# Pooled attention followed by a snake MoE block: transposed layout throughout, batches interleaved, pooling by adds, DMAs from another queue

## The chip, the cores and the metric

One core of one Trainium2 chip. The metric is the device time of one execution in microseconds (us): the median of several executions. The profile is one execution, followed instruction by instruction. Its span runs from the first to the last instruction and is some 2 us shorter than the device time of the same execution.

Engines: PE multiplies matrices, PEld is its weight load, DVE (VectorE), ACT (ScalarE) and POOL (GpSimd) do element work, SP (sync) issues DMAs. Everything is float32.

## The reference

```python
# q, k, v: (8 batches, 8 heads, 576 tokens, 64)
def attn(q, k, v):
    k_p = k.reshape(B, H, 72, 8, 64).mean(axis=3)      # keys and values pooled by 8
    v_p = v.reshape(B, H, 72, 8, 64).mean(axis=3)
    scores = q @ k_p.transpose(0, 1, 3, 2) / sqrt(64)
    scores = scores - scores.max(-1, keepdims=True)
    a = exp(scores)
    a = a / (a.sum(-1, keepdims=True) + 1e-9)
    return a @ v_p

x = attn(q, k, v).transpose(0, 2, 1, 3).reshape(4608, 512)
h = x @ w_in                                            # 512 x 2048
g = h + sin(alpha * h) ** 2 / (alpha + 1e-9)            # alpha: 2048 values, one per column of h
out = g @ w_out                                         # 2048 x 512
```

## The kernel before

Attention runs head by head and query tile by query tile. Each tile is transposed back and written to DRAM; the MoE block reads it again and transposes it on PE, computes h with tokens on the partitions, and transposes h as well, so that the second product can contract over the 2048 columns.

```python
    for b in range(B):
        for h in range(H):
            ...   # loads of k, v, q of 128 tokens, pooling by a matmul with pm, transposes
            for (ms, mlen) in m_tiles:                       # 5 query tiles
                nc.tensor.matmul(sc_ps[:mlen], qt[:, ms:ms + mlen], kp[:], start=True, stop=True)
                ...   # copy, max, exp, sum, reciprocal, multiply: [tokens, 72]
                nc.tensor.transpose(attnT_ps[:, :mlen], attn[:mlen], ident[:mlen, :mlen])
                nc.vector.tensor_copy(out=attnT[:, :mlen], in_=attnT_ps[:, :mlen])
                nc.tensor.matmul(o_ps[:, :mlen], vp[:], attnT[:, :mlen], start=True, stop=True)
                nc.vector.tensor_copy(out=o_sb[:, :mlen], in_=o_ps[:, :mlen])
                nc.tensor.transpose(oT_ps[:mlen, :], o_sb[:, :mlen], ident[:D, :D])
                nc.vector.tensor_copy(out=oT[:mlen], in_=oT_ps[:mlen])
                nc.gpsimd.dma_start(out=x_dram[b, ms:ms + mlen, h, :], in_=oT[:mlen])
    ...   # weights and alpha are loaded here
    for ti in range(NT):                                     # 36 tiles of 128 tokens
        nc.gpsimd.dma_start(out=xc[:], in_=xf[ti * P:(ti + 1) * P, :])
        ...   # four transposes of xc into xT
        for nf in range(n_ff_tiles):
            for kk in range(K1):
                nc.tensor.matmul(h_ps[:], xT[:, kk, :], w_in_t[...], start=(kk == 0), stop=(kk == K1 - 1))
            nc.vector.tensor_copy(out=h_sb[...], in_=h_ps[:])
        for kk in range(K2):                                 # 16
            nc.tensor.transpose(hT_ps[:], h_sb[:, kk * P:(kk + 1) * P], ident[:])
            nc.vector.tensor_copy(out=hT[:], in_=hT_ps[:])
            ...   # sine on ACT, square, times 1/alpha, plus h: three more DVE instructions
            nc.tensor.matmul(out_ps[:], hT[:], w_out_t[:, kk, :], start=(kk == 0), stop=(kk == K2 - 1))
```

Of the kernel before, what the change touches and what calls it, by code (L numbers as in the profile page):

```python
# [13 lines left out]
AF = mybir.ActivationFunctionType  # L15



@with_exitstack
def kernel(  # L20
    ctx: ExitStack,
    tc: tile.TileContext,
    q: bass.AP,
    k: bass.AP,
    v: bass.AP,
    moe_w_in: bass.AP,
    moe_w_out: bass.AP,
    moe_alpha: bass.AP,
    out: bass.AP,
):  # L30
    nc = tc.nc
    B, H, S, D = q.shape
    pool = 8
    Sp = S // pool
    scale = 1.0 / (D ** 0.5)
    d_model = H * D
    N_tok = B * S
    d_ff = moe_w_in.shape[1]
    assert moe_w_in.shape == (d_model, d_ff)
    assert moe_w_out.shape == (d_ff, d_model)  # L40

    x_dram = nc.dram_tensor("x_bridge", (B, S, H, D), F32, kind="Internal").ap()

    P = 128

    singles = ctx.enter_context(tc.tile_pool(name="singles", bufs=1))
    ident = singles.tile([P, P], F32)
    make_identity(nc, ident)
    pm = singles.tile([P, P // pool], F32)
    nc.vector.memset(pm[:], 1.0 / pool)  # L50
    nc.gpsimd.affine_select(out=pm[:], in_=pm[:], pattern=[[-pool, P // pool]],
                            compare_op=mybir.AluOpType.is_ge, fill=0.0,
                            base=0, channel_multiplier=1)
    nc.gpsimd.affine_select(out=pm[:], in_=pm[:], pattern=[[pool, P // pool]],
                            compare_op=mybir.AluOpType.is_ge, fill=0.0,
                            base=pool - 1, channel_multiplier=-1)

    actx = ctx.enter_context(ExitStack())
    apool = actx.enter_context(tc.tile_pool(name="attn_sbuf", bufs=3))
    apsum = actx.enter_context(tc.tile_pool(name="attn_psum", bufs=4, space=bass.MemoryType.PSUM))  # L60

    m_tiles = []
    s0 = 0
    while s0 < S:
        m = min(P, S - s0)
        m_tiles.append((s0, m))
        s0 += m

    n_sc = S // P
    assert S % pool == 0  # L70

    for b in range(B):
        for h in range(H):
            kp = apool.tile([D, Sp], F32)
            vp = apool.tile([Sp, D], F32)
            vp_d = apool.tile([D, Sp], F32)
            qt = apool.tile([D, S], F32)
            off = 0
            sp_off = 0
            while off < S:  # L80
                clen = min(P, S - off)
                clen = (clen // pool) * pool
                kc = apool.tile([P, D], F32)
                vc = apool.tile([P, D], F32)
                qc = apool.tile([P, D], F32)
                nc.gpsimd.dma_start(out=kc[:clen], in_=k[b, h, off:off+clen, :])  # L86
                nc.gpsimd.dma_start(out=vc[:clen], in_=v[b, h, off:off+clen, :])  # L87
                nc.gpsimd.dma_start(out=qc[:clen], in_=q[b, h, off:off+clen, :])  # L88
                qcT_ps = apsum.tile([D, P], F32, tag="ps")
                nc.tensor.transpose(qcT_ps[:, :clen], qc[:clen], ident[:clen, :clen])  # L90
                nc.vector.tensor_copy(out=qt[:, off:off+clen], in_=qcT_ps[:, :clen])
                spc = clen // pool
                kp_ps = apsum.tile([D, P // pool], F32, tag="ps")
                vp_ps = apsum.tile([D, P // pool], F32, tag="ps")
                nc.tensor.matmul(kp_ps[:, :spc], kc[:clen], pm[:clen, :spc], start=True, stop=True)
                nc.tensor.matmul(vp_ps[:, :spc], vc[:clen], pm[:clen, :spc], start=True, stop=True)
                nc.vector.tensor_copy(out=kp[:, sp_off:sp_off+spc], in_=kp_ps[:, :spc])
                nc.vector.tensor_copy(out=vp_d[:, sp_off:sp_off+spc], in_=vp_ps[:, :spc])
                off += clen
                sp_off += spc  # L100
            vpT_ps = apsum.tile([Sp, D], F32, tag="ps")
            nc.tensor.transpose(vpT_ps[:], vp_d[:], ident[:D, :D])
            nc.vector.tensor_copy(out=vp[:], in_=vpT_ps[:])

            for (ms, mlen) in m_tiles:
                sc_ps = apsum.tile([P, Sp], F32, tag="ps")
                nc.tensor.matmul(sc_ps[:mlen], qt[:, ms:ms + mlen], kp[:], start=True, stop=True)  # L107
                sc = apool.tile([P, Sp], F32)
                nc.vector.tensor_copy(out=sc[:mlen], in_=sc_ps[:mlen])
                mx = apool.tile([P, 1], F32)  # L110
# [21 lines left out]
                nc.gpsimd.dma_start(out=x_dram[b, ms:ms + mlen, h, :],  # L132
                                    in_=oT[:mlen])

    actx.close()

    xf = x_dram.rearrange("b s h d -> (b s) (h d)")

# [83 lines left out]
```

## Time and profile before

| | before |
|---|---|
| device time, median | 3109.25 us (3108.4 to 3111.08, 4 runs of the comparison) |
| span of the profile | 3105.1 us |
| busy PE, DVE, ACT, POOL | 66%, 49%, 13%, 23% of the span |
| first stage, attention | to about 1940 us |
| second stage, MoE | 1947 to 3096 us |

A kernel with no engine fully busy can be bound in two ways, and this one has both, one after the other. The average of 66% for PE hides it; the 40 slices of the span, shown in the prediction, do not.

### The profile page before, as it was taken

How to read it: one execution, taken by the hardware profiler on the slowest of the kernel's cores; microseconds unless marked ns; L12 is line 12 of the kernel's file. 1: busy time of each engine (PE TensorE's matmuls, PEld its weight loads, DVE VectorE, ACT ScalarE, POOL GpSimd, SP SyncE). 2: the span in 40 equal slices, each digit the busy share in tenths (PEclk: the TensorE clock that was granted, in tenths of full speed). 3: DMA queues.
4: the chain of work that ended last, by engine and by line, in shares of the span. 5: the costliest groups of instructions: out<-in, count | busy, mean ns of one | idle time of the engine just before them, and what ended most of it. 6: DMA issues, size and time to landing. Idle time of an engine off the chain costs nothing.

```text
span 3105.1 us, 24590 instructions
## 1 busy us (share of the span) xinstructions
PE 2038.2 (66%) x6608; PEld 1024.8 (33%) x6608; DVE 1518.1 (49%) x6214; ACT 408.1 (13%) x1218; POOL 725.8 (23%) x1363
## 2 busy tenths in 40 slices
PE   4444444444444444444444444999999999999998
PEld 2222222222222222222222222344444444444443
DVE  3444444444444444444444443566565656656565
ACT  0100101000000100001000010122121212112121
POOL 4343333333333333333333332000000000000000
PEclk9999999999999999999999999999999999999999
DMA  0000000000000000000000001200000000000000
GB/s 25 17 26 26 20 22 18 22 19 21 20 19 22 17 22 19 21 21 19 23 17 23 19 21 45 89 17 21 14 14 21 14 21 14 21 14 14 21 11 10
DMA packets 48472, 66.66 MB, mean 21 GB/s; under 512 B 21712, under 2 KB 25808, under 8 KB 47824
## 3 DMA queue, kind: packets, MB, share of 16 engines
q0 software_dynamic: 48336, 65.11, 6.5%
q8 instruction: 54, 0.88, 0.1%
q14 instruction: 82, 0.67, 0.1%
HBM read 46.15 MB, written 18.87 MB: 21 GB/s over the span
## 4 chain that ended last, share of the span: by engine, by line
issue 45%; PE 34%; POOL 16%; DVE 3%; DMA 2%; ACT 1%; POOLq 0%
PE out_ps L187 15%; PE h_ps L171 14%; POOL x_bridge L132 5%; POOL kc L86 4%; POOL qc L88 4%; POOL vc L87 3%; PE hT_ps L178 2%; DVE h_sb L173 1%; DMA qc<-in_q_dram 1%; DMA kc<-in_k_dram 1%; PE o_ps L125 0%; DMA w_in_t<-in_moe_w_in_dram 0%; PE sc_ps L107 0%; PE attnT_ps L121 0%; PE xT_ps L164 0%
## 5 line engine op out<-in xcount | busy, mean ns | idle before, releaser
L187 PE MATMUL out_ps<-w_out_t,hT 128*128 128x512 f32 x1152 | 593.8, 629 | 1.1 <-DVE hT L186 0.8
L121 PE MATMUL attnT_ps<-ident,attn 128*72 128x128 f32 (+1 forms) x320 | 130.1, 406 | 626.3 <-DVE attn L119 626.3
L171 PE MATMUL h_ps<-w_in_t,xT 128*128 128x512 f32 x1152 | 515.3, 594 | 12.3 <-DMA w_in_t<-in_moe_w_in_dram 12.3
L132 POOL DMA_DIRECT2D x_bridge<-oT x320 | 173.2, 541 | 989.5 <-DVE oT L131 976.1
L182 ACT ACTIVATE s_t<-hT,alpha_t 128x128 f32<-128x128 f32 x576 | 227.1, 401 | 901.7 <-DVE hT L180 901.7
L171 PEld LDWEIGHTS h_ps<-w_in_t,xT 128*128 128x128 f32 x1152 | 218.0, 192 | 267.5 <-issue 267.3
L112 ACT ACTIVATE mx<-mx 128x1 f32<-128x1 f32 (+1 forms) x320 | 64.9, 203 | 1735.2 <-DVE mx L111 1735.2
L125 PE MATMUL o_ps<-attnT,vp 72*64 72x128 f32 (+1 forms) x640 | 206.4, 426 | 117.3 <-DVE attnT L123 117.3
L121 PEld LDWEIGHTS attnT_ps<-ident,attn 128*72 128x72 f32 (+1 forms) x320 | 43.2, 135 | 691.2 <-DVE attn L119 691.2
L173 DVE COPY h_sb<-h_ps 128x512 f32<-128x512 f32 x144 | 99.5, 691 | 342.3 <-PE h_ps L171 342.2
L187 PEld LDWEIGHTS out_ps<-w_out_t,hT 128*128 128x128 f32 x1152 | 181.2, 188 | 238.2 <-DVE hT L186 201.9
L88 POOL DMA_DIRECT2D qc<-in_q_dram x320 | 171.0, 534 | 230.6 <-PE qcT_ps L90 226.0
L160 POOL DMA_DIRECT2D xc<-x_bridge x36 | 19.6, 543 | 823.7 <-PE xT_ps L164 818.3
L127 DVE COPY o_sb<-o_ps 64x128 f32<-64x128 f32 (+1 forms) x320 | 86.2, 269 | 236.0 <-PE o_ps L125 236.0
L107 PE MATMUL sc_ps<-kp,qt 64*128 64x72 f32 (+1 forms) x640 | 196.9, 410 | 0.0
L129 PE MATMUL oT_ps<-ident,o_sb 64*128 64x64 f32 (+1 forms) x320 | 113.8, 355 | 116.1 <-DVE o_sb L127 116.1
L90 PE MATMUL qcT_ps<-ident,qc 128*64 128x128 f32 (+1 forms) x320 | 124.2, 388 | 90.5 <-DMA qc<-in_q_dram 88.3
L86 POOL DMA_DIRECT2D kc<-in_k_dram x320 | 175.5, 549 | 12.5 <-issue 5.4
L184 DVE TENSOR_TENSOR s_t<-s_t 128x128 f32<-128x128 f32 x576 | 167.7, 291 | 16.6 <-ACT s_t L182 14.2
L117 DVE TENSOR_REDUCE sm<-attn 128x1 f32<-128x72 f32 (+1 forms) x320 | 72.4, 226 | 210.3 <-ACT attn L114 210.3
L186 DVE TENSOR_TENSOR hT<-hT,s_t 128x128 f32<-128x128 f32 x576 | 166.9, 290 | 15.8
L87 POOL DMA_DIRECT2D vc<-in_v_dram x320 | 171.1, 535 | 5.9 <-issue 2.9
(45 smaller groups left out, 2276.5 us busy)
## 6 DMA issues: line engine op xcount, KB each, us to landing
xc<-x_bridge POOLq DMA_DIRECT2D x36, 256.0 KB, 2.9
out_dram<-o_sb POOLq DMA_DIRECT2D x36, 256.0 KB, 2.3
kc<-in_k_dram POOLq DMA_DIRECT2D x256, 32.0 KB, 2.0
vc<-in_v_dram POOLq DMA_DIRECT2D x256, 32.0 KB, 1.9
qc<-in_q_dram POOLq DMA_DIRECT2D x256, 32.0 KB, 1.9
x_bridge<-oT POOLq DMA_DIRECT2D x256, 32.0 KB, 1.7
w_in_t<-in_moe_w_in_dram POOLq DMA_DIRECT2D x1, 4096.0 KB, 13.5
w_out_t<-in_moe_w_out_dram POOLq DMA_DIRECT2D x1, 4096.0 KB, 22.0
```

The lines of the kernel that those rows point to most:

```text
L86: nc.gpsimd.dma_start(out=kc[:clen], in_=k[b, h, off:off+clen, :])
L87: nc.gpsimd.dma_start(out=vc[:clen], in_=v[b, h, off:off+clen, :])
L88: nc.gpsimd.dma_start(out=qc[:clen], in_=q[b, h, off:off+clen, :])
L107: nc.tensor.matmul(sc_ps[:mlen], qt[:, ms:ms + mlen], kp[:], start=True, stop=True)
L121: nc.tensor.transpose(attnT_ps[:, :mlen], attn[:mlen], ident[:mlen, :mlen])
L125: nc.tensor.matmul(o_ps[:, :mlen], vp[:], attnT[:, :mlen], start=True, stop=True)
L132: nc.gpsimd.dma_start(out=x_dram[b, ms:ms + mlen, h, :], in_=oT[:mlen])
L171: nc.tensor.matmul(h_ps[:], xT[:, kk, :], w_in_t[:, kk, nf * N_FF_TILE:(nf + 1) * N_FF_TILE], start=(kk == 0), stop=(kk == K1 - 1))
L182: nc.scalar.activation(out=s_t[:], in_=hT[:], func=AF.Sin, bias=0.0, scale=alpha_t[:, kk:kk + 1])
L184: nc.vector.tensor_mul(out=s_t[:], in0=s_t[:], in1=s_t[:])
L186: nc.vector.tensor_add(out=hT[:], in0=hT[:], in1=s_t[:])
L187: nc.tensor.matmul(out_ps[:], hT[:], w_out_t[:, kk, :], start=(kk == 0), stop=(kk == K2 - 1))
```

## The change

Its intent: keep the features on the partitions from attention to the end of the MoE block, so that nothing has to be transposed back or sent through DRAM; do attention for a whole batch at once; and put the attention of batch b+1 between the MoE steps of batch b, so that its latency lies under PE's matmuls. Pooling becomes three adds of halves, on GpSimd (DVE for the first batch's keys). DMAs are issued from sync.

The diff rewrites the file; its core:

```diff
-    for b in range(B):
-        for h in range(H):
-            ...
-            for (ms, mlen) in m_tiles:
-                ...
-                nc.tensor.transpose(oT_ps[:mlen, :], o_sb[:, :mlen], ident[:D, :D])
-                nc.gpsimd.dma_start(out=x_dram[b, ms:ms + mlen, h, :], in_=oT[:mlen])
+        # pooling: 8 -> 4 -> 2 -> 1 by adds
+        for n, eng in (("k", nc.vector if b == 0 else nc.gpsimd), ("v", nc.gpsimd)):
+            for i, t in enumerate(st[n]):
+                for w in (4 * D, 2 * D, D):
+                    eng.tensor_tensor(out=o, in0=t[:, :, 0:w], in1=t[:, :, w:2 * w], op=OP.add)
+        yield
+        # two heads per score matmul, by block-diagonal keys kb
+        for i, (t0, n) in enumerate(tiles):
+            for g in range(2):
+                for hh in range(2):
+                    nc.tensor.matmul(..., qt[:, hp, t0:t0 + n], kb[:, hp, :], start=True, stop=True)
+                ...   # max and subtract on DVE
+                yield
+        nc.scalar.activation(out=ex[:, 0:4], in_=ex[:, 0:4], func=AF.Exp, scale=scale)
+        nc.scalar.activation(out=ex[:64, 4], in_=ex[:64, 4], func=AF.Exp, scale=scale)
+        ...   # sums and reciprocals on DVE, multiply on GpSimd, transposes, copies
+        # output of attention, transposed: features on the partitions
+            for hp in range(NP):
+                for e in range(2):
+                    h = 2 * hp + e
+                    nc.tensor.matmul(ps[64 * e:64 * e + 64, :n], vp[:, h, :], aT[:, h, t0:t0 + n], start=True, stop=True)
+                nc.vector.tensor_copy(out=self.xT[c][:, hp, o:o + n], in_=ps[:, :n])
+                yield
-    for ti in range(NT):
-        nc.gpsimd.dma_start(out=xc[:], in_=xf[ti * P:(ti + 1) * P, :])
-        ...
-        for kk in range(K2):
-            nc.tensor.transpose(hT_ps[:], h_sb[:, kk * P:(kk + 1) * P], ident[:])
-            ...
+    def moe(self, c):                                  # a chunk of 384 tokens
+        for f in range(K2 + 2):
+            if f < K2:
+                for kk in range(K1):
+                    nc.tensor.matmul(ps[:], self.w_in_t[:, kk, f * P:(f + 1) * P], xT[:, kk, :], ...)
+                nc.scalar.activation(out=s[:], in_=ps[:], func=AF.Sin, scale=self.al[:, f:f + 1])
+                nc.scalar.activation(out=s[:], in_=s[:], func=AF.Square)
+                nc.vector.scalar_tensor_tensor(out=g[:], in0=s[:], scalar=self.ral[:, f:f + 1], in1=ps[:], ...)
+            if f >= 2:
+                for t in range(NT):
+                    nc.tensor.matmul(acc[t][:], gs[f - 2][:, t * P:(t + 1) * P], self.w_out_t[:, f - 2, :], ...)
+            yield
+            for cc in chunks:
+                for _ in self.moe(cc):
+                    for _ in range(4 if len(chunks) == 1 else 2):
+                        next(nxt, None)                # a piece of the next batch's attention
```

Below, an "f step" is one turn of the loop over f: 8 records of h and 6 of the output. A record is one entry of PE in the trace; a float32 matmul leaves two, a transpose one.

## The prediction

> **What bounds the kernel now.** I read the slices of the span first (busy tenths of each engine in 40 slices), then the table of stretches, then one tile of each stage in the timeline.
>
> ```profile
> PE   4444444444444444444444444999999999999998
> DVE  3444444444444444444444443566565656656565
> POOL 4343333333333333333333332000000000000000
> ```
>
> There are two stages one after the other: attention up to about 1940 us, in which no engine is half busy, and the MoE block, in which the PE has no gap. The table of stretches gives the same in numbers (busy us of each engine in 400 us of each stage):
>
> ```profile
> 1200.00:1600.00 400.00, 189.63 (x754) 111.27 (x754) 168.49 (x753) 37.35 (x134) 142.05 (x267) 1.00 0.06 20
> 2000.00:2400.00 400.00, 393.82 (x1056) 171.67 (x1055) 251.04 (x925) 80.48 (x204) 13.54 (x25) 1.00 0.05 17
> ```
>
> Attention, one query tile of one head in the timeline (start, duration, engine, what, and the idle time before it):
>
> ```profile
> 1011.81 0.20 ACT L112 ACTIVATE mx<-mx 128x1 f32<-128x1 f32 x1 [4.06 <-DVE mx L111]
> ...
> 1013.21 0.43 PE L121 MATMUL attnT_ps<-ident,attn 128*72 128x128 f32 x1 [1.96 <-DVE attn L119]
> 1013.67 0.29 DVE L123 COPY attnT<-attnT_ps 72x128 f32<-72x128 f32 x1 [0.52 <-PE attnT_ps L121]
> 1014.02 0.69 PE L125 MATMUL o_ps<-attnT,vp 72*64 72x128 f32 x2 [0.38 <-DVE attnT L123]
> 1014.74 0.28 DVE L127 COPY o_sb<-o_ps 64x128 f32<-64x128 f32 x1 [0.78 <-PE o_ps L125]
> 1015.08 0.36 PE L129 MATMUL oT_ps<-ident,o_sb 64*128 64x64 f32 x1 [0.37 <-DVE o_sb L127]
> ...
> 1016.00 0.55 POOL L132 DMA_DIRECT2D x_bridge<-oT  x1 [4.09 <-DVE oT L131]
> ...
> 1016.46 0.20 ACT L112 ACTIVATE mx<-mx 128x1 f32<-128x1 f32 x1 [4.05 <-DVE mx L111]
> ```
>
> It is a relay: each instruction starts when the one before has ended on another engine. The same step recurs 4.65 us later (1011.81 to 1016.46). 320 tiles x 4.65 = 1488 us; the remaining 450 us are 64 head openings of 7 us (loads, pooling, q transposes). So attention is latency, not work.
>
> MoE, steady state:
>
> ```profile
> 2499.83 0.19 PEld L171 LDWEIGHTS h_ps<-w_in_t,xT 128*128 128x128 f32 x1 [0.24 <-issue]
> 2500.26 0.19 PEld L171 LDWEIGHTS h_ps<-w_in_t,xT 128*128 128x128 f32 x1 [0.24 <-issue]
> 2500.69 0.19 PEld L171 LDWEIGHTS h_ps<-w_in_t,xT 128*128 128x128 f32 x1 [0.24 <-issue]
> ...
> 2513.77 0.27 PE L178 MATMUL hT_ps<-ident,h_sb 128*128 128x128 f32 x1
> 2513.88 1.12 PE L187 MATMUL out_ps<-w_out_t,hT 128*128 128x512 f32 x2
> ...
> 2514.83 0.27 PE L178 MATMUL hT_ps<-ident,h_sb 128*128 128x128 f32 x1
> ```
>
> One weight load per 0.43 us, so a record of 512 columns takes 0.43 us of the PE, and an fp32 matmul is two records. A step of the second half (one transpose and one matmul) recurs after 1.06 us: 0.86 for the matmul, about 0.2 for the transpose (0.11 of it streaming, the rest the change between transpose and matmul). Check: 2304 records x 0.43 = 991, 720 transposes x 0.21 = 151, sum 1142 us; the stage from the arrival of the weights (1947) to the last matmul (3096) is 1149.
>
> **What the skill says.** (1) "FP8 and Floating Point Precision", section "TensorE Precision Notes": true FP32 takes 4 passes through the array. With the 2.4 GHz of "TensorE: Matmul & The Clock Gate", section "Back-to-back issue gap", 512 x 2 / 2.4 = 0.427 us a record: the trace agrees (0.43, granted clock 1.00). So 384 columns should take 0.32 us a record. (2) "GPSIMD Engine Reference", section 3.1: a two-input fp32 add of 2048 elements takes 4497 ns there, 2.2 ns an element, about twice the VectorE. The trace has no such instruction, so this is unchecked. (3) "ScalarE: Activation LUTs", section "What ACT_TABLE_LOAD costs": a switch of set is a load of 1283 ns and a drain of about the same. The trace has the 1.28 us load, but only twice; the change has 28.
>
> **The change, part by part.**
>
> *Matmuls of the MoE: unchanged in columns.* h: 768 matmuls of 384 columns (two records of 0.32) = 495 us. Output: 576 of 512 columns (0.86) = 495 us. Sum 990 us, which no part of the change makes smaller. I take this as the floor.
>
> *MoE transposes, bridge and reloads: gone.* 720 transposes (151 us of PE) and the copies that fed them, 36 reloads, and 320 writes of the bridge.
>
> *Attention work on the PE, per batch.* 64 transposes in 16 groups: 64 x 0.107 + 16 x 0.1 for the change of kind = 8.5 us. 20 score matmuls of 144 columns with two heads at once (block-diagonal keys): streaming would be 0.24, but two weight loads must be hidden behind it; the small matmuls of before take 0.33 a pair, so I take 0.30, 6.0 us. Attention times v: 8 x 576 columns x 4 / 2.4 GHz = 7.7 us. Sum 22 us, seven batches under the MoE: 155 us. This replaces 1940 us of relay.
>
> *Opening.* Batch 0 still runs alone. k and v are 2.4 MB, in 10 us (the weights ran at near 400 GB/s before); q is 4608 rows of 256 bytes, whose rate I can only bracket: the page of before gives 67 ns of an engine per packet on average, 288 packets an engine, hence at most 19 us; I take 14. q is complete near 24. Scores: 10 groups x (reduce + subtract of 288 elements, 0.46 each by the 0.69 of a 512 copy less 224 elements) = 10 us. Exp of 2304 and 576 elements 3 us, sums 2, five multiplies on GpSimd at 1.4 us = 7, last transposes 1, attention times v 5 and a copy, waits 3. MoE starts near 55 us. The weights (8.4 MB, 22 us after q) and alpha land near 47, just in time.
>
> *Stalls while interleaved.* The instruction order shows scores, exp, normalisation and transposes of the next batch placed between f steps (5.2 us of matmuls each), with loads and pooling one or two batches ahead. The chain from the last score to the first transpose is about 8 us (subtract 0.9, table load 1.3, exp 2.1, sums 1.5, reciprocal 0.4, multiply 1.4, handovers), against 5 us of matmuls placed between: 3 us a batch, plus a little for three PSUM buffers: 4 x 7 = 30 us.
>
> *Tail and launch:* last copies and output DMA (2.3 us before) 4 us; time less span, 3110 - 3105 = 5 us.
>
> Sum: 990 + 155 + 55 + 30 + 9 = 1239 us.
>
> *Other engines.* ACT: 192 x (sine 0.61 + square 0.51) = 215, eight batches x 11 of copies and exp = 88, table loads 36 (72 with drains), outputs 8: near 370 us. DVE: 192 x 0.56 + 8 x 23 + 24 x 0.69 = 310. POOL: per batch 7168 adds x 2.2 ns = 16 plus multiplies 7, 180 us. None is a third as long as the PE.
>
> **Rivals.** (a) *The relay moves into the PE's own queue.* The PE is in order, so a transpose that waits for exp and GpSimd stops the MoE behind it. For it: 16 groups a batch, each waiting for another engine. Against: an f step of 5 us between most of them, far above the 0.3 to 0.7 us hops of the trace. At 15 us a batch: 1310. (b) *GpSimd or DMA late.* Pooling of batch 1 can start only after batch 0's multiplies and after the weights have landed; if its adds take twice the 2.2 ns, the key transposes of batch 1 stop the PE for about 8 us, and the opening grows by 7. 1260. (c) *Table switches and exp block the sines.* Each block is about 7 us on ACT; two h buffers give about 8 us of slack. If both exps pay a pair of switches, up to 5 us a batch: 1270. (d) *The two 64-column halves of attention times v run side by side in the array*, and stalls are small: minus 27 and minus 15: 1195.
>
> **Range and chances.** 1239 with (a) to (c) on one side and (d) on the other: 1195 to 1310. To miss a 2% gain, nearly all the relay would have to survive: 1%.
>
> **What would show it.** Right: the two-stage picture is gone; after an opening near 55 us the PE slices are all 9; h records 0.32 us apart; POOL and ACT below 40%; the chain of waits nearly all PE. Wrong on the floor: records further apart than 0.32 and 0.43, or a granted clock below 1. Wrong on stalls: a list of waits in which PE's waits for DVE, ACT or POOL (ps_at, ps_kt) come to more than 50 us. Wrong on the opening: first h matmul after 65 or before 45 us.

## More of the kernel before

A table of stretches gives the busy time of each engine (columns: stretch, its length, then busy us and number of instructions of PE, PEld, DVE, ACT, POOL, then granted PE clock, DMA share and GB/s).

```profile
2510.00:2515.00 5.00, 5.00 (x15) 1.80 (x13) 4.76 (x20) 2.01 (x5) 0.00 (x0) 1.00 0.01 3
```

PE is full, and DVE is busy 95% as well: in this part of the second stage two engines are at their limit together.

## The result, and the profile after

| | before | after |
|---|---|---|
| device time, median | 3109.25 us | 1168.53 us (1167.95 to 1170.32, 4 runs) |
| span of the profile | 3105.1 us | 1166.6 us |
| busy PE, DVE, ACT, POOL | 66, 49, 13, 23% | 98, 26, 27, 15% |

The ratio is 0.3759, with a 95% interval of 0.3754 to 0.3765. Ratios here are the mean time of one kernel's fast runs over that of the other's in the same rounds, so not quite the ratio of the medians. The prediction said 1239 with a range from 1195: the direction was right, the time was 70 us lower and below the range.

The same slices of the span as before, with PE's granted clock in tenths:

```profile
PE   4899999999999999999999999999999999999998
...
POOL 3597421011021122102000100010000100000000
PEclk9899999999999999999999999999999999999999
```

The two stages are gone: one slice of opening, one mixed, then a full PE to the end. A table of stretches shows how full:

```profile
60.00:1160.00 1100.00, 1099.11 (x3594) 587.17 (x3593) 273.57 (x559) 301.87 (x499) 147.89 (x112) 1.00 0.11 28
```

Of 1100 us, PE is busy 1099, at full clock; DVE and ACT need about a quarter of it. The chain of work that ended last says the same, first before, then after:

```profile
issue 45%; PE 34%; POOL 16%; DVE 3%; DMA 2%; ACT 1%; POOLq 0%
```

```profile
PE 95%; DVE 2%; SPq 1%; POOL 1%; ACT 1%; DMA 0%; issue 0%; POOLq 0%; ACTq 0%
```

Pieces of that chain, after, give the length of a chunk (columns: start, duration, what). Each line is the last 18 records of a chunk:

```profile
140.00 7.72 PE acc L202 x18
...
322.85 7.72 PE acc L202 x18
...
423.38 7.72 PE acc L202 x18
...
1072.65 7.73 PE acc L202 x18
...
1155.13 7.74 PE acc L202 x18
```

The last two chunks have no attention beside them: 1155.13 - 1072.65 = 82.48 us each, twelve of which are 989.8 us. From 140.00 to 322.85 two chunks hold one batch's attention: 182.85, which is 17.9 more than two bare chunks; from 322.85 to 423.38 one chunk holds one: 100.53, which is 18.05 more. So a batch's attention costs 18.0 us, and 7 of them 126 us.

The list of PE's waits over the whole span (us in total, times, longest), after:

```profile
PE ps_kt L112 <- DVE kp L106: 11.1, 2, 8.8
PE ps_at L160 <- POOL ex L154: 5.9, 5, 4.8
PE ps_qt L121 <- DMA qm<-in_q_dram: 3.5, 2, 3.3
...
```

and the same list from 60 us on, which has one line:

```profile
PE ps_at L160 <- POOL ex L154: 0.8, 3, 0.3
```

Nearly all the waiting is in the opening. In the 1107 us after it PE waited 0.8 us for another engine. The timeline of one interleaved softmax (batch 2) shows why (start, duration, engine, what, and the idle time before it):

```profile
189.72 1.29 PE L137 MATMUL ps_sc<-kblk,qt 128*128 128x144 f32 x8
...
193.23 2.12 ACT L145 ACTIVATE ex<-ex 128x2304 f32<-128x2304 f32 x1
...
195.39 1.41 DVE L151 TENSOR_REDUCE sm<-ex 128x8 f32<-128x576 f32 x2 [3.16 <-ACT ex L145]
...
196.29 0.70 PE L137 MATMUL ps_sc<-kblk,qt 128*64 128x144 f32 x4
...
198.24 2.25 POOL L154 TENSOR_TENSOR ex<-ex,sm 128x576 f32<-128x576 f32 x2 [34.06 <-DVE sm L153]
...
202.18 0.60 PE L160 MATMUL ps_at<-ident,ex 128*72 128x128 f32 x4
```

The first transpose is at 202.18 and needs only the first of the two multiplies that start at 198.24, of 1.15 us each. It also doesn't need the scores of the last, short query tile at 196.29, because exp is issued as two instructions, tiles 0 to 3 and tile 4. So between the last scores that it needs (189.72) and the transpose lie 12.5 us, of which 10.6 are the matmuls of two f steps, and the chain takes about 10 of them (to 199.4, the end of the first multiply). In every second batch (that of 362.3, for one) only 8.6 us of MoE matmuls lie between; the three waits of 0.3 us are in those batches.

The opening, in the timeline of PE:

```profile
34.92 6.29 PE L160 MATMUL ps_at<-ident,ex 128*72 128x128 f32 x32 [4.81 <-POOL ex L154]
...
42.35 3.45 PE L178 MATMUL ps_o<-aT,vp 72*64 72x384 f32 x24 [0.23 <-ACT aT L162]
45.73 0.91 PE L193 MATMUL ps_h<-xT,w_in_t 128*128 128x384 f32 x2
```

The scores end at 30.1, where the idle time of the first line begins: normalisation keeps PE waiting 4.8 us; then the transposes and attention times v follow, and the first h starts at 45.73.

### The profile page after: what moved, and what is told of

Same layout as the page of the kernel before. It is cut to its first block, busy times and chain, and to the rows that moved or that the text cites. A ratio compares the mean times of both kernels' runs of the same rounds, so it can differ in the third digit from the quotient of the medians.

```text
span 1166.6 us, 9629 instructions
## 1 busy us (share of the span) xinstructions
PE 1139.9 (98%) x3776; PEld 612.6 (53%) x3776; DVE 304.9 (26%) x624; ACT 316.2 (27%) x520; POOL 175.8 (15%) x138
## 4 chain that ended last, share of the span: by engine, by line
PE 95%; DVE 2%; SPq 1%; POOL 1%; ACT 1%; DMA 0%; issue 0%; POOLq 0%; ACTq 0%
PE ps_h L193 42%; PE acc L202 42%; PE ps_sc L137 3%; PE ps_o L178 3%; PE ps_at L160 2%; PE ps_qt L121 1%; SPq L93 1%; POOL ex L154 1%; DVE sm L151 1%; ACT ex L145 0%; DVE mx L140 0%; DMA qm<-in_q_dram 0%; DVE ex L141 0%; PE ps_qr L126 0%; PE ps_kt L112 0%
## 5 line engine op out<-in xcount | busy, mean ns | idle before, releaser
L193 PE MATMUL ps_h<-xT,w_in_t 128*128 128x384 f32 x1536 | 532.1, 489 | 0.0
L202 PE MATMUL acc<-w_out_t,g 128*128 128x512 f32 x1152 | 524.2, 593 | 0.0
L193 PEld LDWEIGHTS ps_h<-xT,w_in_t 128*128 128x128 f32 x1536 | 283.7, 190 | 206.9 <-issue 35.4
L202 PEld LDWEIGHTS acc<-w_out_t,g 128*128 128x128 f32 x1152 | 217.6, 190 | 235.5 <-issue 188.4
L195 ACT ACTIVATE s<-ps_h,al 128x384 f32<-128x384 f32 x192 | 111.4, 580 | 651.0 <-PE ps_h L193 650.8
L198 DVE SCALAR_TENSOR_TENSOR g<-s,ral,ps_h 128x384 f32<-128x384 f32 x192 | 117.4, 612 | 621.3 <-ACT s L196 615.9
L106 POOL TENSOR_TENSOR kvin<-kvin 72x1024 f32<-72x1024 f32 (+1 forms) x60 | 108.0, 1805 | 50.3 <-DMA kvin<-in_v_dram 25.9
L196 ACT ACTIVATE s<-s 128x384 f32<-128x384 f32 x192 | 100.4, 523 | 5.8
L154 POOL TENSOR_TENSOR ex<-ex,sm 128x576 f32<-128x576 f32 (+1 forms) x40 | 45.2, 1147 | 369.8 <-DVE sm L152 196.9
L137 PE MATMUL ps_sc<-kblk,qt 128*128 128x144 f32 (+1 forms) x320 | 50.2, 296 | 1.9 <-DVE ex L141 1.9
```

Source lines behind the costliest of these rows:

```text
L106: eng.tensor_tensor(out=o, in0=t[:, :, 0:w], in1=t[:, :, w:2 * w], op=OP.add)
L137: nc.tensor.matmul(ps[:n, 2 * hh:2 * hh + 2, :].rearrange("p h k -> p (h k)"), qt[:, hp, t0:t0 + n], kb[:, hp, :], start=True, stop=True)
L154: nc.gpsimd.tensor_tensor(out=ex[:n, i], in0=ex[:n, i], in1=sm[:n].unsqueeze(2).to_broadcast([n, H, Sp]), op=OP.mult)
L193: nc.tensor.matmul(ps[:], self.w_in_t[:, kk, f * P:(f + 1) * P], xT[:, kk, :], start=(kk == 0), stop=(kk == K1 - 1))
L195: nc.scalar.activation(out=s[:], in_=ps[:], func=AF.Sin, scale=self.al[:, f:f + 1])
L196: nc.scalar.activation(out=s[:], in_=s[:], func=AF.Square)
```

## The experiments

All kernels ran on chips of one kind, with the kernel before beside them; its median was between 3104.8 and 3107.7 in every group. Where nothing else is said, a kernel is the changed kernel with the one edit shown, it gave the right result, and a time stands against 1168.5.

### The terms of the sum

**No attention of batches 1 to 7** (`e5_floor`: every chunk computes on the first chunk's input). Its output is wrong, which doesn't matter for the time.

```diff
-        xT = self.xT[c]
+        xT = self.xT[0]
-                st[b + 1] = self.load_batch(b + 1)
-                nxt = self.attention(b + 1, st[b + 1])
+                nxt = iter(())
```

> Wrong results on purpose: only batch 0 has its attention, all twelve MoE chunks use the first chunk's x. Theory (a MoE chunk costs 82.5 us of dense matmuls, and attention of seven batches adds just its PE time of 18 us each): 47 opening + 990 + 6 = 1042 us, so seven batches of attention cost 126 us. Rival (the floor itself is lower or higher than 990 because ACT or DVE set the pace of a chunk): more than 6 us away from 1042.

Measured: 1042.20 us (ratio 0.3354). The seven attentions therefore cost 1168.5 - 1042.2 = 126.3 us, the 7 x 18.0 read off the trace, where the prediction had 155 plus 30 of stalls.

**Attention times v over all 128 columns** (`e1_av_full`). The values of a head get zeros in the other head's 64 columns, and the two matmuls of a pair of heads add into one output. It is the same number of matmuls and of streamed columns; only the two cannot lie side by side. (GpSimd also gets the zeros and a split last add to do; PE's waits from 60 us on stayed at 0.8 us, so that does not show in the steady part; before, at 56 us, PE waited 2.3 us for it once.)

```diff
-                    nc.tensor.matmul(ps[64 * e:64 * e + 64, :n], vp[:, h, :], aT[:, h, t0:t0 + n], start=True, stop=True)
+                    nc.tensor.matmul(ps[:, :n], vp[:, h, :], aT[:, h, t0:t0 + n], start=(e == 0), stop=(e == 1))
```

> Attention times v with each head's v widened to 128 zero-padded columns, so that the two heads of a pair are two full-array matmuls added up in one PSUM tile, and cannot lie side by side in the array. Same columns streamed. Theory (the two 64-column halves run at the same time in the changed kernel, 4.4 us a batch instead of the 7.7 that I had summed): the eight batches lose 3.3 to 3.9 us each, 1195 to 1200 us. Rival (the halves do not overlap, the saving against my sum lies elsewhere): within 4 us of 1168.5.

Measured: 1196.11 us (ratio 0.3849), 27.6 more, over all eight batches. From 60 us on, where seven of them are, attention times v took PE 30.8 us in the changed kernel and 55.1 here, start to next start: 24.3 of the 27.6; the rest lies in the first 60 us, with the first h at 50.7 instead of 45.7. The two 64-column halves do run at the same time, as the prediction's rival (d) had it. The trace of the changed kernel shows it directly, in a stretch in which 16 records, 4 of 192 columns and 12 of 384, precede an h group:

```profile
391.35 2.48 PE L178 MATMUL ps_o<-aT,vp 72*64 72x192 f32 x16
...
393.77 0.91 PE L193 MATMUL ps_h<-xT,w_in_t 128*128 128x384 f32 x2
```

One after the other, at the trace's 0.32 us per 384 columns, these would take 4 x 0.16 + 12 x 0.32 = 4.5 us; they took 2.42, and record by record they start in pairs 7 ns apart. "TensorEngine Tiling (Array Packing)", section "When to Use Tiling", of the Trainium skill names this case: with 64 stationary columns the array can be used as two column tiles. The trace agrees, here for float32.

**One exp that waits for all five tiles** (`e2_late_exp`). A zero bias, computed from the last score, makes the large exp wait for the short tile.

```diff
+        nc.vector.tensor_scalar(out=z[:64], in0=mx[:64, 0:1], scalar1=0.0, scalar2=None, op0=OP.mult)
-        nc.scalar.activation(out=ex[:, 0:4], in_=ex[:, 0:4], func=AF.Exp, scale=scale)
+        nc.scalar.activation(out=ex[:, 0:4], in_=ex[:, 0:4], func=AF.Exp, scale=scale, bias=z[:, 0:1])
```

> The exp of query tiles 0 to 3 is tied to the last score (its bias is a zero made from the last maximum), as my prediction had counted it, so the chain from the last score to the first transpose is whole. Theory (there was no stall because the first transposes depend on tiles 0 to 3 only and stand two f steps, 11 us of matmuls, behind their score; the order built for this kernel will again place them where they are ready): PE waits below 10 us in all, 1168 to 1176 us, the opening a microsecond or two longer. Rival (my prediction: 8 us of chain against 5 us of matmuls): 3 us a batch, 1185 to 1195 us.

Measured: 1173.26 us (ratio 0.3775), 4.7 more. The first h came at 48.3 instead of 45.7, so 2.6 of this is the opening; PE's waits from 60 us on were 1.9 us instead of 0.8. Even without the split exp the interleaved stalls are nowhere near the predicted 30 us: the scheduler, which orders the instructions when the kernel is built, put 8.3 us of MoE matmuls between the short tile's scores and the first transpose, where the changed kernel has 3.1 to 5.3.

**Attention pieces handed out faster** (`e3_rate12`): 12 pieces per f step instead of 2 or 4, so that fewer matmuls lie between a producer and its consumer.

```diff
-                    for _ in range(4 if len(chunks) == 1 else 2):
+                    for _ in range(12):
```

> Twelve attention steps are written after each f step in place of four or two, so the next attention is packed into the first few f steps of a batch, and the chains of softmax have little matmul work between their links. Theory (stalls are absent in the changed kernel because 11 us of matmuls stand between a score and its transposes): PE's waits for DVE, ACT and POOL come back, 2 to 8 us a batch, 1180 to 1220 us. Rival (the scheduler spreads the steps by itself, whatever rate is written): within 5 us of 1168.5.

Measured: 1173.95 us (ratio 0.3778), 5.4 more. PE's waits for GpSimd's multiply from 60 us on rose from 0.8 to 10.8 us (15 times). This lies between the two expectations. The waits that the prediction feared do appear when matmuls are taken from between, but the scheduler still spreads the pieces, and they come to 1.5 us a batch. The time grew by less than the waits, because the packed pieces cost PE some 4 us less elsewhere (start to next start).

**No interleaving** (`e4_apart`): the same code, with `range(0)`, so that in the program each batch's attention stands by itself. The scheduler still moves a few of its pieces (key and q transposes at 172.6 lie between h groups).

> No interleaving in the program: the whole next attention is written after the MoE chunks of the batch; only the scheduler's own look-ahead may overlap them. Theory (batched attention alone is short: the opening shows 25 us from the first q transposes to the MoE, of which 18 are PE work): 8 to 15 us more for each of seven batches, 1225 to 1275 us; the PE's waits for DVE, ACT and POOL become 60 to 100 us. Rival (interleaving is what brings the attention from 1940 us down): 7 x 25 or more, above 1340 us.

Measured: 1250.16 us (ratio 0.4023), 81.6 more. The list of PE's waits from 60 us on:

```profile
PE ps_at L160 <- POOL ex L154: 47.0, 14, 6.2
PE ps_sc L137 <- DVE ex L141: 13.4, 28, 0.5
```

That is 60 us of waits, with a few more from shorter lines. The mean granted clock fell from 0.997 to 0.974: after a wait of 6.15 us the next 16 transposes took 3.6 us, twice what they take in a stream. So interleaving in the program is worth 82 us here, three quarters of them waits of PE.

**Twice the squares on ACT** (`e6_act_double`): a second square per f step, written to a tile that nobody reads, 100 us of work in all.

> One more Square per f step whose result nobody uses: 192 x 0.52 = 100 us more work on ACT (316 to 416 us), in the same queue as the sines. Theory (the PE is full and ACT has slack): 1168 to 1172 us. Rival (ACT's queue decides when the g tiles come, so its time shows): plus 30 to 100 us.

Measured: 1167.89 us (ratio 0.3760). ACT has room; its 28 table loads of 1.28 us are hidden as well.

**Pooling on DVE only** (`e8_pool_dve`).

```diff
-        for n, eng in (("k", nc.vector if b == 0 else nc.gpsimd), ("v", nc.gpsimd)):
+        for n, eng in (("k", nc.vector), ("v", nc.vector)):
```

> All pooling adds on VectorE in place of GpSimd (this part of the change undone: 7168 adds a batch at about 1.2 ns an element, 8 us a batch more on DVE, which then is near 370 us busy). Theory (PE full, DVE has slack): 1166 to 1176 us; GpSimd's 2.3 ns an element never mattered. Rival (the adds hold up the g tiles in DVE's queue): plus 20 us or more.

Measured: 1170.87 us (ratio 0.3769), 2.3 more. GpSimd's part in the pooling is off the path; what little it saves shows as PE's waits for the softmax (waits for the multiply from 60 us on 3.6 instead of 0.8 us).

**All DMAs from GpSimd again** (`e7_swdge`): `nc.sync` replaced by `nc.gpsimd` in every load and store of the changed kernel.

> All DMAs of the changed kernel issued from GpSimd again (this part of the change undone). Theory (the issue engine matters in the opening only; there the five q loads took 13 us to issue from sync; from GpSimd an issue took 0.5 us before, but GpSimd also sets up its tiles and the pooling waits behind the issues): 1160 to 1180 us, and the steady part unchanged. Rival (GpSimd's queue, in order, holds back pooling and normalisation behind DMA issues that wait for buffers, so the PE waits in the steady part too): 1200 us and more.

Measured: 1186.78 us (ratio 0.3815); the profiled run took 1179.6. The expectation was missed. The steady part did not change (waits from 60 us on: 0.8). The opening did: first h at 55.95, 10.2 us later. It is not the time of the issues, which took GpSimd 4.3 us for the five q loads against 13.3 on sync. Some 3.5 us are a later start: the first load was issued at 2.26 instead of 0.73, behind GpSimd's setup of its tiles, and the scores began at 24.5 instead of 21.1. The list of DVE's waits between 30 and 60 us has the reason for most of the rest:

```profile
DVE ral L77 <- DMA al<-in_moe_alpha_dram: 7.7, 1, 7.7
```

The instruction that prepares 1/alpha stood in DVE's queue ahead of the softmax sums, and waited for alpha; PE in turn waited 6.5 us for DVE. The timed runs had a mean clock of 0.986 against 0.994 in the profiled one, which fits their being 7 us longer; they have no trace, so where the clock was low stays open.

### Where the saving came from

**The kernel before with its DMAs from sync** (`e9_before_sync`): one word in ten lines.

> The kernel before with every DMA issued from sync instead of GpSimd: that part of the change alone. Theory (attention is a relay of 4.65 us a tile in which the bridge's writes are not links; only the head openings, where k, q, v chunks are issued in turn at 0.5 us each, can get shorter): 0 to 250 us less, 2860 to 3100 us. Rival (an issue from sync takes as long or is held behind the bridge's writes in one queue): 3100 us or more.

Measured: 3093.69 us against 3107.06, ratio 0.9957. The issuing engine is worth 13 us of the 1941.

**The kernel before with the transposed MoE block alone** (`e11_moe_only`). Attention is left tile by tile, but writes its output, transposed, into a tile on chip; the MoE block is the new one.

```diff
-                nc.tensor.transpose(oT_ps[:mlen, :], o_sb[:, :mlen], ident[:D, :D])
-                ...
-                nc.gpsimd.dma_start(out=x_dram[b, ms:ms + mlen, h, :], in_=oT[:mlen])
+                nc.vector.tensor_copy(out=xT_all[64 * e:64 * e + 64, h // 2, b * S + ms:b * S + ms + mlen],
+                                      in_=o_ps[64 * e:64 * e + 64, :mlen])
```

> The other half of the change alone: the attention of the kernel before, per head and tile as it was, but its transposed output copied straight into an on-chip x and the transposed MoE of the changed kernel behind it; no bridge, no MoE transposes, no interleaving, no batching. Theory (the MoE falls from 1150 to 990 plus 15 us of weights, the relay loses only the last transpose, about 0.2 to 0.5 us of 4.65 a tile): 1780 to 1880 + 1010 = 2790 to 2890 us, so batching and interleaving are worth over 1600 of the 1940 us saved. Rival (the on-chip hand-over itself is the gain): below 2500 us.

Measured: 2722.51 us (ratio 0.8764), 68 us below the expected range. The missed part is the relay: without the transpose back, its copy and its store, a query tile recurs after 4.08 us instead of 4.65,

```profile
999.94 0.23 DVE L112 TENSOR_REDUCE mx<-sc 128x1 f32<-128x72 f32 x1
...
1004.03 0.23 DVE L112 TENSOR_REDUCE mx<-sc 128x1 f32<-128x72 f32 x1
```

which is 320 x 0.56 = 180 us. The head openings gave another 50: attention ends at 1699.5 instead of 1928.9. The MoE stage, first h to last output matmul, went from 1149 to 1002 us. So of the 1941 us, about 385 come from the layout and 1554 from doing attention a batch at a time and under the matmuls. The run without interleaving, at 1250, splits these: some 1470 us for attention a batch at a time (with its new loads and pooling), 82 for the interleaving.

**The kernel before with its output matmul two steps behind its transpose** (`e13_before_ahead`).

```diff
-        for kk in range(K2):
+        for kk in range(K2 + 2):
+            if kk < K2:
                 nc.tensor.transpose(hT_ps[:], h_sb[:, kk * P:(kk + 1) * P], ident[:])
                 ...
-            nc.tensor.matmul(out_ps[:], hT[:], w_out_t[:, kk, :], ...)
+            if kk >= 2:
+                nc.tensor.matmul(out_ps[:], hTs[kk - 2][:], w_out_t[:, kk - 2, :], ...)
```

> The kernel before with its second MoE half written two blocks ahead (transpose of block k+2 ahead of the output matmul of block k), to find what the extra 0.1 us per transpose was that I charged to a change between transpose and matmul. In the changed kernel four transposes between matmuls take 0.43 us and nothing more. Theory (in the kernel before the output matmul's weights, hT, come late from DVE, and their load is exposed; with two blocks ahead it is prefetched): 576 x 0.1 = 58 us less, near 3050 us. Rival 1 (DVE, four operations of a block in 1.06 us, sets the pace): within 15 us of 3107. Rival 2 (the change of kind costs 0.1 whatever the order): within 15 us too, but DVE would then have gaps.

Measured: 3100.60 us, ratio 0.9981. The theory of a hidden wait was wrong; the time is where both rivals had it. A step still recurs after 1.07 us, and its stretch reads as that of the kernel before did:

```profile
2508.00:2513.00 5.00, 5.00 (x15) 1.90 (x13) 4.59 (x19) 2.00 (x5) 0.00 (x0) 1.00 0.00 0
```

PE is shown full and DVE busy 92%. The expectation's sign of Rival 2 was that DVE has gaps. In 2507 to 2518 us of the kernel before, DVE never stood still for more than 0.04 us; here it has a gap of 0.12 us in every second step. That leans to Rival 1, DVE's pace, for the kernel before, but no run changed DVE's work alone, so it is not shown. The changed kernel, which doesn't transpose h, relieves both.

### The opening

The opening was 9 us shorter than predicted, and these runs ask what sets its length.

**The changed kernel again** (`e14_after_again`), no edit.

> The changed kernel itself, so that the next two can be set against it on one chip in the same rounds. Expected 1167.5 to 1170.5 us, as before; anything beyond 1171 would say that differences of 2 us between runs of different sessions mean nothing.

Measured: 1168.54 us (ratio 0.3760), 0.01 from the first session. Differences of 2 us between medians can be read.

**q of the first batch issued from two queues** (`e10_q_split`).

```diff
-            nc.sync.dma_start(out=qm[:n, i], ...)
+            eng = nc.scalar if b == 0 and i < 3 else nc.sync
+            eng.dma_start(out=qm[:n, i], ...)
```

> Only the first batch's q loads differ: three of the five tiles are issued from ScalarE's queue instead of sync's, which has 13.3 us of issuing to do for five of them. Theory (the opening is set by q's issue): the two queues issue side by side, about 8 us instead of 13.3, q is complete near 10 to 13 us instead of 18, the first h matmul starts near 39 to 42 instead of 45.7, and the time is 1162 to 1166 us. Rival (the opening is set by the transfer of q's 4608 short rows, or by what follows it): q lands at the same time and the time stays within 2 us of the changed kernel.

Measured: 1171.85 us (ratio 0.3770), 3.3 more: the theory fell, and the rival's 2 us were exceeded too. The issuing itself was faster (4.3 us on ACT and 8.0 on sync side by side), but q was complete no earlier: its last 256-byte row moved at 18.3 us by the DMA records (18.7 in the changed kernel of these rounds). The second tile's transpose waited until 16.78, and the last tiles' until 21.16, where PE's order had put them behind the keys; the scores began at 24.6 instead of 21.2. This is what "DMA: Bandwidth & Descriptors", section "Issuing engines are not separate DMA queues", says: all queues share the same 16 DMA engines, and two issuers save only the issuing. Here k and v, 2.4 MB, go through the same engines before or beside q either way.

**The split issue, q ahead of v, and the first batch in two parts** (`e12_open_split`): scores to attention times v for the first 384 tokens, then the first MoE chunk, with the other 192 tokens between its f steps. Here tiles 0, 2 and 4 of q are issued from ScalarE.

```diff
+        parts = [(tiles[:3], 0, 384), (tiles[3:], 384, self.S)] if b == 0 else [(tiles, 0, self.S)]
+        for some, lo, hi in parts:
             ...   # scores, exp, normalisation, transposes, attention times v of these tiles
-        for _ in self.attention(0, st[0]):
-            pass
+        first = self.attention(0, st[0])
+        for w in first:                  # up to the end of the first part
+            if w:
+                break
```

> Both possible causes of the opening's length removed at once: q of the first batch issued from two queues, and the first batch's attention in two parts, the first 384 tokens before the first MoE chunk and the other 192 between the steps of that chunk. Theory (9 of the opening's 46 us are the relay of all five tiles before the first chunk may start): first h matmul near 31 to 36 us, the time 1150 to 1161 us, and at least 4 us below the run with the split issue alone. Rival (the relay only moves: the second part stops PE inside the first chunk for as long as it saved): first h near 33 but PE waits of 6 us or more for exp, GpSimd or alpha in the first 150 us, and a time within 3 us of the run with the split issue alone.

Measured: 1170.90 us (ratio 0.3766), 1.0 below the run with the split issue alone and 2.4 above the changed kernel. The first h came at 35.7, ten us earlier than in the changed kernel, and nothing was gained. (The profiled run was the quickest of the four, 1168.35; the clock of the others was 0.993 instead of 0.995.) The timeline of PE:

```profile
42.65 1.13 PE L210 MATMUL ps_h<-xT,w_in_t 128*128 128x384 f32 x3
45.88 1.74 PE L176 MATMUL ps_at<-ident,ex 128*72 128x128 f32 x16 [2.10 <-POOL ex L170]
47.85 1.55 PE L193 MATMUL ps_o<-aT,vp 72*64 72x192 f32 x16 [0.23 <-ACT aT L178]
51.28 4.54 PE L210 MATMUL ps_h<-xT,w_in_t 128*128 128x384 f32 x8 [1.87 <-DVE g L215]
```

After two h groups the third had to wait until 51.28 for the first g, whose sine ran at 49.11 only: both buffers of h were full. PE filled a part of the time with the second part's transposes and attention times v, and stood still for 4.2 us. ACT's list of waits has none for alpha in this stretch: in its queue the sines simply stood behind the second part's exps and copies. The scheduler had put them there; alpha's load was last in the queue, behind 8.4 MB of weights. Alpha itself had arrived by then: the DMA records of its four-byte words lie between 36 and 43 us.

**Alpha loaded first** (`e16_alpha_early`), from GpSimd's queue, otherwise the changed kernel.

```diff
+        # at the start
+            nc.gpsimd.dma_start(out=self.al[:], in_=self.alpha.rearrange("(k p) -> p k", p=P))
-        # behind the weights
-            nc.sync.dma_start(out=self.al[:], in_=self.alpha.rearrange("(k p) -> p k", p=P))
```

> The changed kernel with one edit: alpha, 2048 words, is loaded first, from GpSimd's queue, instead of last behind 8.4 MB of weights. In the changed kernel alpha was ready at about 49 us, when the first h had just ended (first h at 45.7 to 46.0), so alone it should be worth nothing: 1166.5 to 1170 us. Rival (alpha holds the changed kernel's opening as well): 2 us or more faster, below 1166.5.

Measured: 1169.63 us (ratio 0.3768): nothing by itself, as expected. The 49 us of the expectation, and of the next one, are misread: that is when the first instruction read alpha. In the changed kernel, too, alpha's words had moved by 42 us.

**The split opening with alpha first** (`e15_split_alpha`): both edits above.

> The split opening with alpha loaded first. Theory: in the split opening the first h matmul was early (35.7 us) but alpha came at 49.1, so PE stood idle and the gain was lost; with alpha early the next thing late is the second batch's pooled keys, which GpSimd finished at 51.5 and 55.9 us there. First h near 35 to 37, the waits for alpha gone (the first sine near 40), PE waits for GpSimd's pooled keys of 3 to 9 us, and a time of 1162 to 1168 us. Rival (the split opening gains nothing because its PE work and its lower clock cost what it saves): 1169 us or more although alpha is early.

Measured: 1164.48 us (1163.90 to 1164.87, 5 runs; ratio 0.3750, 0.3745 to 0.3755), 5.1 below the run with alpha alone in the same rounds. The theory holds in its main step: the first sine ran at 41.0 and the stop before the third h group is gone. Two details of the expectation were wrong. The wait for the second batch's keys did not come (the scheduler placed them later, at 65.1), and the first h came at 38.1, not 35 to 37. Of the 2.4 us to the split opening before it, 1.0 had come up by the first scores (18.1 against 17.1), 0.8 in the scores, and 0.6 from the transposes on, where PE ran slowly for longer:

```profile
30.00:35.40 5.40, 5.34 (x26) 4.33 (x28) 2.64 (x5) 1.97 (x4) 2.25 (x3) 0.50 1.05 387
```

Granted clock 0.50, after a wait of 6 us for GpSimd; 24 transposes took 5.3 us. After the first h, PE did 5.4 us of the second part's work (the groups of the timeline, start to next start), of which 0.8 came after the first h in the run with alpha alone too. Its first h was at 46.7, so 8.6 - 4.6 = 4.0 us were to be gained, and the span is 4.3 shorter. This is the fastest version found.

**The second batch's keys pooled on DVE as well** (`e17_split_alpha_k1`).

```diff
-        for n, eng in (("k", nc.vector if b == 0 else nc.gpsimd), ("v", nc.gpsimd)):
+        for n, eng in (("k", nc.vector if b <= 1 else nc.gpsimd), ("v", nc.gpsimd)):
```

> As the run before, and the pooling of the second batch's keys on VectorE as well (in the changed kernel only the first batch's are). Its load landed by 46.9 us in the split opening, and VectorE takes 4.7 us for it, so the keys are ready near 52 instead of 56. PE waits in the first 100 us outside the first 30 below 3 us, and the time is 1160 to 1165: first h 10 us earlier than in the changed kernel, less about 5 us of the first batch's second part that PE now does after that point. Rival (the loads of the second batch themselves are late): no faster than the run before.

Measured: 1165.79 us (ratio 0.3755), 1.3 more than the run before, and 0.8 us outside the expected range. There was no wait to remove, and PE now waited 1.2 us for these keys from DVE.

## Why the prediction was wrong in size and right in kind

Its sum, term by term:

| term of the prediction | predicted | measured | how |
|---|---|---|---|
| MoE matmuls, the floor | 990 | 989.8 | 12 x 82.48 from the chain |
| attention on PE, seven batches | 155 | 125.5 | 126.3 without the stalls |
| stalls while interleaved | 30 | 0.8 | list of waits from 60 us on |
| opening to the first h | 55 | 45.7 | timeline |
| tail and launch | 9 | 5.5 | 3.7 from the last matmul to the end of the span, 1.8 time less span of the same run |
| sum | 1239 | 1167.3 | the profiled run took 1168.4, the median 1168.5 |

1. **What bounds the kernel before: right.** Latency in attention, PE in the MoE stage. What the prediction missed, and no number rested on, is that DVE is within some per cent of its limit in the second half of the MoE stage (95% busy; the output matmul two steps behind gained 0.2%).
2. **The floor: right to 0.2 us**, since it was counted in records of 0.43 us that the trace of before showed. Records of 384 columns came 0.322 us apart. (With the 0.32 that the prediction prints, h would be 491.5 and not 495; the last 0.2 us are luck.)
3. **Attention on PE: the step that failed is "8 x 576 columns x 4 / 2.4 GHz = 7.7 us" for attention times v.** It took the two halves of a pair one after the other, and put their overlap among the rivals as (d), "minus 27". The run with full columns measured 24.3 us for it in these seven batches. The diff showed each half writing to its own 64 partitions; nothing in the profile of before had such a pair, so the trace could not decide it, but the tiling page quoted above would have been the reason to expect it. A batch's pieces, start to next start: attention times v 4.4 us (predicted 7.7), transposes 6.7 (8.5), scores 5.4 (6.0). Four transposes of a group took 0.43 us (207.78 to 208.21), with no extra 0.1 for the change of kind. The pieces make 16.5; the other 1.4 of a batch's 17.9 are lost in the matmuls next to them.
4. **Stalls: the step that failed is "8 us from the last score to the first transpose, against 5 us of matmuls placed between".** It took the short fifth tile as the start of the chain. The first transpose does not depend on it; behind the scores that it needs lie 10.6 us of MoE matmuls (8.6 in every second batch), and PE waited 0.8 us in all where 30 had been predicted. Making exp wait for the fifth tile as well brought only 1.9 us of waits in the steady part, because the scheduler then put 8.3 us behind that tile; only handing out pieces faster (10.8 us) or not interleaving at all (over 60 us) brings the stalls back. So rival (a) is a real mechanism, with a margin that the order of instructions keeps.
5. **The opening: all three of its pieces were too long.** q was complete 24 us in by the prediction; the last of it was transposed at 20.4, and the scores began at 21.1. The scores took 9 (predicted 10). From there to the first h the prediction added up 21 us as if each stage ran to its end; they pipeline tile by tile and took 15.6 (30.1 to 45.7). A cost that it left out went the other way: after the 4.8 us wait PE's clock was at half for about 5 us. Two stretches of the changed kernel's opening, 36 to 38 and 42 to 44 us:

```profile
36.00:38.00 2.00, 2.00 (x11) 1.74 (x10) 1.75 (x6) 0.85 (x2) 0.84 (x1) 0.50 1.04 385
42.00:44.00 2.00, 1.77 (x13) 0.77 (x12) 1.07 (x3) 1.58 (x2) 0.00 (x0) 1.00 0.52 159
```

   "TensorE: Matmul & The Clock Gate", Part 1, has the gate fall to half after an idle window of about 3.4 us and rise again after a busy one; the trace agrees in kind: the granted clock was 0.50 from 33.2 us, 3.1 us into the wait, to 40.05, then 1.00. The transposes in the slow stretch took 6.29 us for 32, 0.20 each against 0.107.
6. **Tail and launch: 3.5 us too long.** The 5 us of launch were the span of one run taken from the time of another; a run of the kernel before shows 1.7 between the two (3106.14 and 3104.4).
7. **Rivals (b) and (c) did not happen.** GpSimd's largest adds took 2.3 ns an element where 2.2 was estimated, and neither doubled ACT work (no change) nor pooling moved to DVE (2.3 us) was on the path.
8. **The range.** Its low end, 1195, was (d) at minus 27 and half of the stalls at minus 15, with everything else at its estimate (which makes 1197). (d) came nearly as sized (24), all of the stalls went (minus 29), and the opening and the tail added 12.8 us on the same side. The estimates of stalls and opening had each been put at the cautious end, and a range around their sum has to allow for that.

What stays open: why the timed runs with all DMAs from GpSimd had a lower clock than their profiled run, and which of PE and DVE is the first limit in the second half of the old MoE stage (its trace leans to DVE).

## What to carry to other kernels

When a latency-bound stage can be cut into pieces that lie between matmuls of another stage, ask for each piece only how much independent PE work stands between its last needed input and its consumer: here 8.6 to 10.6 us of MoE matmuls stood over a chain of 10, with small pieces of attention between, and the whole relay of seven batches cost 0.8 us of waiting. Count PE work by what the array can do at once, not by columns alone: two matmuls into different 64-column halves cost little more than one (30.8 us against 55.1). And an opening has several walls close behind each other (q, the softmax of five tiles, the order of the sines, the clock after a wait), so removing one of them alone gained nothing or lost 3 us, and removing several together gained 4.

## What the Trainium skill lacked or had wrong

- "TensorE: Matmul & The Clock Gate", section "Back-to-back issue gap", gives a sustained spacing of about 131 ns for 512 columns and calls the 216 ns of its formula an over-count. Here, in float32, 18 records of 512 columns took 7.72 us; at two passes a record that is 0.214 us a pass, with PE full for 1100 us. The formula holds for this stream, and no run came near 131.
- The same page, "Part 4: PE-mode transpose", gives about 275 ns for a transpose in a kernel and says that the full clock does not engage for transposes. As the length of one record that agrees (273 ns), but in a stream four transposes took 0.43 us, 0.107 each. And the clock did engage: in the opening PE did nothing but transposes from 34.92 to 42 us, and the granted clock went from 0.50 to 1.00 at 40.05.
- "TensorEngine Tiling (Array Packing)", section "When to Use Tiling", names two 64-column tiles but gives no measured float32 case. Here the pairing is worth 24.3 us over seven batches of 32 such records each, 8 x 576 columns a batch.
- "DMA: Bandwidth & Descriptors" doesn't say for how long a load holds the queue that issues it. Five loads of q with 4608 rows of 256 bytes held sync's queue for 13.3 us and GpSimd's for 4.3; with the issue split, three of them held ScalarE's queue for 4.3 and the other two sync's, behind k and v, for 8.0. So it isn't the shape alone. Alpha, 2048 words, held sync's for 5.1 to 7.7.
- "ScalarE: Activation LUTs", section "What ACT_TABLE_LOAD costs", adds a drain of about 1380 ns to each load of 1283. The load is as stated; no such drain shows: an exp ended at 195.35 and the next load began at 195.37, and that exp had begun at 193.23, when its own load (191.94, 1.28 us) had just ended.
- No page says that a load's place in the queue also moves the consumers' place in another engine's instruction order: with alpha last, the sines of the split opening stood behind exps that did not need it, and PE's third h group waited until 51.28 us without any wait for alpha in the trace.
